# Scores of a head pair in one group, with two banks taken from the general PSUM pool

## The chip, the cores and the metric

The kernel runs on one core of one Trainium2 chip. The metric is the device time of one execution in microseconds (us), and every time below is the median of several executions unless it says otherwise. PE is TensorE, PEld its weight loads, DVE VectorE, ACT ScalarE, POOL GpSimd, SP SyncE. L469 means line 469 of the kernel concerned; the change shifts the lines.

## The reference

Two operators in a row: causal attention with a decay ("forgetting attention"), then a two-layer network with the SiLU function.

```python
def _attn_ref(q, k, v, f):                 # q, k, v: (8, 8, 576, 64); f: (8, 8, 576)
    scores = scale * np.matmul(q, k.transpose(0, 1, 3, 2))
    cum = np.cumsum(np.log(np.clip(f, 0.0001, 1.0)), axis=-1)
    decay = cum[:, :, :, None] - cum[:, :, None, :]
    scores = np.where(causal, -1000000000.0, scores + decay)
    ...                                    # softmax over the last axis
    return np.matmul(attn, v)

def _moe_ref(x, w_in, w_out):              # x: (4608, 512), w_in: (512, 2048), w_out: (2048, 512)
    h = x @ w_in
    g = h * (1.0 / (1.0 + np.exp(-h)))
    return g @ w_out
```

The output is 4608 x 512 in float32.

## The kernel before

The attention runs in 16 rounds of two units each; a unit is a pair of heads of one batch element. In between, slots are filled with pieces of the network, which make up most of the PE work. A piece is either an **M1** chunk (four matmuls into an `hp` tile, then tanh on ACT into `th`, then a multiplication on DVE into `gt`) or an **M2** part (four matmuls `po` that read finished `gt`). Two pools share the eight PSUM banks that the kernel uses: `psc` has two tiles of two banks for the scores, `pbig` has four tiles of one bank for everything else.

```python
psc  = tc.tile_pool(name="psc",  bufs=2, space=PSUM)   # [P, 2, 512] fp32: two banks each
pbig = tc.tile_pool(name="pbig", bufs=4, space=PSUM)   # one bank each: hp, po, dn, tx

def scores(n, c):                        # unit n, chunk c of 0, 1, 2
    ...
    sc = psc.tile([P, 2, SM], FP32, name="sc", tag="sc")
    for kb, q0, q1, o in CHUNKS[c]:
        for i in range(2):               # two heads: two 64-row halves of PE
            ...
            nc.tensor.matmul(sc[:, i, o : o + q1 - q0], lhsT=kt, rhs=t[r, q0:q1], ...)
    w = SM if c < 2 else T0
    nc.scalar.activation(out=u[:, :, c * SM : c * SM + w], in_=sc[:, :, 0:w], func=ACT.Exp, ...)
    ...                                  # masks on DVE; chunk 2 has a second exponential, into ut

def attend(n):                           # exponentials times values
    dn = pbig.tile([P, NGR, D + 1], FP32, name="dn", tag="big")
    ...

for m in range(NQ):                      # 16 rounds, two units each
    n = 2 * m
    piece = 1.7 if m < 2 else 2.4
    scores(n, 0); scores(n, 1); prepare(n)
    slot(piece, 2)                       # about 2.4 us of M1 and M2 pieces, M2 first if there is one
    ...                                  # back(m - 1): turn the attention output
    scores(n, 2); scores(n + 1, 0); prepare(n + 1)
    slot(piece, 2)
    scores(n + 1, 1); scores(n + 1, 2)
    slot(piece, 2)
    attend(n); attend(n + 1)
    slot(min(3.5, max(0.8, behind() - LAG)) if m > 1 else 0.8, 1)
```

(Calls that stand on lines of their own are put together here.) M2 of a token group can only run behind M1 of the same group, so now and then the M2 pieces run dry, and a slot then holds only `hp`.

The softmax here doesn't subtract the row's maximum and nothing guards it: scores larger than these inputs give would overflow.

## Time and profile before

| | before |
|---|---|
| median time | 346.49 us (three runs, 346.45 to 346.81) |
| span of the profiled run | 344.3 us |
| start, before the attention loop is in full swing | to about 58 us |
| loop of 16 rounds | about 58 to 284 us |
| tail, M1 and M2 only | from about 284 us |

Here are busy times by stretch for the loop, in us. The columns are the stretch, its length, then busy time and number of instructions for PE, PEld, DVE, ACT and POOL, then the granted PE clock, the share of the DMA engines in use and GB/s.

```profile
76.00:134.00 58.00, 56.37 (x696) 34.82 (x694) 35.53 (x76) 41.47 (x77) 28.07 (x47) 1.00 0.94 185
134.00:190.00 56.00, 56.00 (x662) 32.66 (x659) 32.96 (x66) 39.04 (x70) 21.85 (x38) 1.00 0.93 177
190.00:284.00 94.00, 93.76 (x1061) 56.28 (x1058) 51.65 (x113) 63.07 (x118) 26.53 (x47) 1.00 0.67 132
```

PE is busy for 206.13 of 208 us, ACT for 143.58 (69%). In the whole stretch from 134 to 190 us PE shows no idle time at all.

### The profile page before, as it was taken

Reading aid. Unit: us, or ns where it says so; the run is one execution under the profiler, and the core shown is the slowest. Engines: PE = TensorE matmul, PEld = TensorE weight load, DVE = VectorE, ACT = ScalarE, POOL = GpSimd, SP = SyncE. Lnnn points to the kernel's source line nnn. Section 1 sums busy time; section 2 is a strip of 40 time slices with the busy share of each in tenths; the row PEclk is TensorE's granted clock in tenths of the full one; section 3 lists DMA queues with packets and bytes.
Section 4 is the critical chain, followed back from the end, with each engine's and each line's share of the span. In section 5 each row is a group of like instructions: output and inputs, shape, how many; then the busy total and the mean of one; then the engine's idle time right before and its main releaser. Section 6 shows DMA issues by size and latency. Waiting matters only on the chain.

```text
span 344.3 us, 8892 instructions
## 1 busy us (share of the span) xinstructions
PE 335.4 (97%) x3567; PEld 198.9 (58%) x3567; DVE 185.5 (54%) x389; ACT 218.1 (63%) x401; POOL 129.0 (37%) x227
## 2 busy tenths in 40 slices
PE   8999999999998999999999999999999999999995
PEld 3654656667655656466465665656656565555654
DVE  4766646465667466367547653547645454535330
ACT  5866654887585766756759567595775934445341
POOL 8996225824427273055137128225320000010011
PEclk9999999999999999999999999999999999999999
DMA  8999999999699899798889999989832000010103
GB/s 157 200 185 220 198 163 162 236 214 194 159 186 197 202 202 159 169 191 182 166 205 153 171 195 196 154 182 197 147 86 56 33 32 30 32 55 30 40 38 86
DMA packets 141497, 50.44 MB, mean 147 GB/s; under 512 B 132368, under 2 KB 138768, under 8 KB 141456
## 3 DMA queue, kind: packets, MB, share of 16 engines
q1 hardware_dynamic: 131440, 32.70, 53.3%
q0 software_dynamic: 9856, 17.04, 21.4%
q8 instruction: 28, 0.46, 0.6%
q10 hardware_dynamic: 160, 0.13, 0.1%
q14 instruction: 13, 0.11, 0.1%
HBM read 36.85 MB, written 9.44 MB: 134 GB/s over the span
## 4 chain that ended last, share of the span: by engine, by line
PE 74%; DMA 13%; POOL 4%; SPq 3%; ACT 2%; DVE 2%; issue 1%; POOLq 0%
PE po L613 31%; PE hp L568 29%; PE sc L460 6%; PE dn L507 5%; DMA w_out_bf<-in_moe_w_out_dram 3%; DMA vf<-in_v_dram 3%; PE dn L516 3%; DMA qktf<-in_k_dram 3%; DMA qkT<-qkb 2%; SPq L158 1%; DMA f_sb<-in_f_dram 1%; DMA kf<-in_k_dram 1%; ACT th L576 1%; SPq L168 1%; ACT u L464 1%
## 5 line engine op out<-in xcount | busy, mean ns | idle before, releaser
L576 ACT ACTIVATE th<-hp 128x384 bf16<-128x384 f32 (+2 forms) x208 | 96.0, 478 | 90.6 <-PE hp L568 88.3
L577 DVE SCALAR_TENSOR_TENSOR gt<-th,hp 128x384 bf16<-128x384 bf16 (+2 forms) x208 | 105.9, 521 | 79.4 <-ACT th L576 75.8
L613 PE MATMUL po<-w_out_bf,gt 128*128 128x512 bf16 (+1 forms) x592 | 144.7, 374 | 0.0
L568 PE MATMUL hp<-x,w_in_bf 128*128 128x384 bf16 (+2 forms) x704 | 128.9, 321 | 0.2
L568 PEld LDWEIGHTS <-w_in_bf 128*128 128x128 bf16 x832 | 78.5, 98 | 55.2 <-issue 2.2
L613 PEld LDWEIGHTS <-gt 128*128 128x128 bf16 x592 | 54.6, 98 | 49.6 <-issue 2.1
L464 ACT ACTIVATE u<-sc 128x1024 bf16<-128x1024 f32 (+1 forms) x96 | 75.1, 821 | 11.1 <-PE sc L460 10.9
L592 POOL DMA_DIRECT2D out_dram<-osb x38 | 21.0, 552 | 133.4 <-ACT osb L623 86.4
L414 POOL TENSOR_TENSOR vp<-vf,w_bf 128x520 bf16<-128x520 f32 (+1 forms) x32 | 34.0, 1064 | 28.3 <-DMA vf<-in_v_dram 27.4
L469 DVE TENSOR_TENSOR u<-u,tri 128x768 bf16<-128x768 bf16 x32 | 22.6, 707 | 18.4 <-ACT u L464 18.4
L483 DVE TENSOR_TENSOR ut<-ut,trit 128x128 bf16<-128x128 bf16 x32 | 11.3, 354 | 34.8 <-ACT ut L476 34.8
L400 POOL CAST qkb<-qf 128x384 bf16<-128x384 f32 x32 | 17.3, 542 | 33.5 <-DMA qf<-in_q_dram 32.7
L623 ACT ACTIVATE osb<-po 128x512 f32<-128x512 f32 (+1 forms) x37 | 22.0, 594 | 12.4 <-PE po L613 12.3
L460 PE MATMUL sc<-qkT 64*128 64x128 bf16 (+1 forms) x640 | 26.5, 207 | 1.1 <-DMA qkT<-qkb 0.8
L460 PEld LDWEIGHTS <-qkT 64*128 64x128 bf16 x640 | 18.2, 94 | 12.2 <-issue 8.1
L476 ACT ACTIVATE ut<-sc 128x640 bf16<-128x640 f32 x32 | 23.3, 727 | 0.0
L507 PEld LDWEIGHTS <-u 128*128 128x128 bf16 x576 | 20.7, 97 | 3.9 <-issue 1.6
L507 PE MATMUL dn<-vp,u 128*128 128x65 bf16 x384 | 21.8, 193 | 0.0
L507 PE MATMUL dn<-v,u 128*128 128x65 bf16 x192 | 19.8, 193 | 1.3 <-DVE gt L577 1.3
L525 DVE TENSOR_TENSOR xr<-dn,rec 128x448 bf16<-128x448 f32 x32 | 20.0, 624 | 1.1
L400 POOL CAST qkb<-kf 128x384 bf16<-128x384 f32 x32 | 17.4, 543 | 7.9 <-DMA kf<-in_k_dram 7.8
L568 PE MATMUL hp<-xt,w_in_bf 128*128 128x256 bf16 x128 | 18.2, 272 | 0.3 <-DVE gt L577 0.2
(68 smaller groups left out, 204.5 us busy)
## 6 DMA issues: line engine op xcount, KB each, us to landing
out_dram<-osb POOLq DMA_DIRECT2D x32, 256.0 KB, 3.1
vf<-in_v_dram SPq DMA_DIRECT2D x26, 256.0 KB, 4.9
qf<-in_q_dram SPq DMA_DIRECT2D x64, 96.0 KB, 2.9
kf<-in_k_dram SPq DMA_DIRECT2D x64, 96.0 KB, 2.8
w_in_bf<-in_moe_w_in_dram POOLq DMA_DIRECT2D x4, 512.0 KB, 6.8
w_out_bf<-in_moe_w_out_dram POOLq DMA_DIRECT2D x4, 512.0 KB, 9.6
vf<-in_v_dram POOLq DMA_DIRECT2D x6, 256.0 KB, 10.0
qkb<-in_q_dram POOLq DMA_DIRECT2D x8, 128.0 KB, 5.0
```

What stands on the lines that cost most here:

```text
L400: nc.gpsimd.tensor_copy(out=t2[:, c0 : c0 + NR, :].rearrange("p c x -> p (c x)"), in_=t[:, :, :, :].rearrange("p c h d -> p (c h d)"),)
L414: nc.gpsimd.tensor_tensor(out=vbf[b][r, c, :, :], in0=vst[b][c][r, :, :], in1=w_bf[r, c + 1, b * H : (b + 1) * H, None].to_broadcast([n, H ...
L460: nc.tensor.matmul(sc[:, i, o : o + q1 - q0], lhsT=kt, rhs=t[r, q0:q1], start=True, stop=True)
L464: nc.scalar.activation(out=u[:, :, c * SM : c * SM + w], in_=sc[:, :, 0:w], func=ACT.Exp, scale=scale)
L469: nc.vector.tensor_tensor(out=x, in0=x, in1=tri[:, None, None, :].to_broadcast([P, 2, NR, P]), op=ALU.mult,)
L476: nc.scalar.activation(out=ut[:, :, 0:3:2, :].rearrange("p k i t -> p i k t"), in_=sc[:, :, T0 : T0 + (NM + 1) * ST].rearrange("p i (k t) ...
L507: nc.tensor.matmul(dn[:, i * NR + c - 1, :], lhsT=u[:, i, o : o + P], rhs=vals(kb, i), start=(kb == 0), stop=(kb == c),)
L568: nc.tensor.matmul(hp[:, :], lhsT=w_in_bf[:, cc, fc * P : (fc + 1) * P], rhs=xcols(g, cc), start=(cc == 0), stop=(cc == NCC - 1),)
L576: nc.scalar.activation(out=th[:, :], in_=hp[:, :], func=ACT.Tanh, scale=0.5)
L577: nc.vector.scalar_tensor_tensor(out=gt[:, fc, :], in0=th[:, :], scalar=1.0, in1=hp[:, :], op0=ALU.add, op1=ALU.mult,)
L613: nc.tensor.matmul(po[:, :], lhsT=gt[:, fc, tb * P : (tb + 1) * P], rhs=w_out_bf[:, fc, m0:m1], start=(fc == 0), stop=(fc == NFC - 1),)
L623: nc.scalar.activation(out=osb[:, :], in_=po[:, :], func=ACT.Copy, scale=0.5)
```

## The change

Its intent: fewer interruptions of the PE stream. The three chunks of one unit's scores are issued as one group, so two units make two groups where they made three. One group needs six banks (two for each chunk); the score pool has four, so chunk 1 takes two tiles of the general pool. Its exponential is split in two, one for each bank. The exponentials of chunk 2 are held back (`late`) until after the next M1 piece, so that its tanh comes first. The attention output `dn` moves from the general pool into the score banks. The slots are set to begin and end with an M2 piece where there is one. The diff, cut to its core:

```diff
-    def scores(n, c):
+    late: list = []
+    def scores(n):
...
-        sc = psc.tile([P, 2, SM], FP32, name="sc", tag="sc")
-        for kb, q0, q1, o in CHUNKS[c]:
+        for c in range(3):
+            if c == 1:
+                sc[c] = [pbig.tile([P, SM], FP32, name="sb", tag="big") for _ in range(2)]
+            else:
+                sc[c] = psc.tile([P, 2, SM], FP32, name="sc", tag="sc")
...
+            if c == 1:
+                for i in range(2):
+                    nc.scalar.activation(
+                        out=u[:, i, SM : 2 * SM], in_=sc[c][i][:, :], func=ACT.Exp, scale=scale
+                    )
+        def rest():
...                                     # both exponentials of chunk 2 and the mask of ut
+        late.append(rest)
@@ attend
-        dn = pbig.tile([P, NGR, D + 1], FP32, name="dn", tag="big")
+        dn_ = psc.tile([P, 2, SM], FP32, name="dn", tag="sc")
+        dn = dn_[:, 0, 0 : NGR * (D + 1)].rearrange("p (c d) -> p c d", d=D + 1)
@@ step
             m1_chunk(*M1[a])
+            while late:
+                late.pop(0)()
@@ fill
+            if last:
+                force = first if not begun else (last if at["left"] < 900 else 0)
+            t = step(force)
@@ the loop of 16 rounds
-        piece = 1.7 if m < 2 else 2.4
-        scores(n, 0)
-        scores(n, 1)
+        piece = 2.2 if m < 2 else 3.4
+        scores(n)
         prepare(n)
-        slot(piece, 2)
+        slot(piece, 2, 2)
...
-        scores(n, 2)
-        scores(n + 1, 0)
+        scores(n + 1)
         prepare(n + 1)
-        slot(piece, 2)
-        scores(n + 1, 1)
-        scores(n + 1, 2)
-        slot(piece, 2)
+        slot(piece, 2, 2)
         attend(n)
+        slot(0.7, 1)
         attend(n + 1)
-        slot(min(3.5, max(0.8, behind() - LAG)) if m > 1 else 0.8, 1)
+        slot(min(3.0, max(0.6, behind() - LAG)) if m > 1 else 0.6, 1, 2)
```

More of the change, by code (lines that the diff above doesn't have):

```diff
@@ L443 @@
     AT |= {(2, 1): RB, (3, 1): SM + RB, (3, 2): 2 * SM}
-    def scores(n, c):
+    late: list = []
+    def scores(n):
         b, p = divmod(n, NP)
-        if c == 0:
-            us[n] = upool.tile([P, 2, UW], BF16, name="u", tag="u")
+        us[n] = upool.tile([P, 2, UW], BF16, name="u", tag="u")
         u, ut = us[n], uts[n % 4]
         t = qkT[n]
-        sc = psc.tile([P, 2, SM], FP32, name="sc", tag="sc")
-        for kb, q0, q1, o in CHUNKS[c]:
-            for i in range(2):
-                r = slice(i * D, (i + 1) * D)
-                if kb == 0:
-                    kt = kT0[b][r, p, :]
-                else:
-                    k0 = RB if kb == NM else kb * P + RB
-                    kt = t[r, k0 : k0 + P]
-                nc.tensor.matmul(
-                    sc[:, i, o : o + q1 - q0], lhsT=kt, rhs=t[r, q0:q1], start=True, stop=True
-                )
-        w = SM if c < 2 else T0
-        nc.scalar.activation(
-            out=u[:, :, c * SM : c * SM + w], in_=sc[:, :, 0:w], func=ACT.Exp, scale=scale
-        )
-        if c == 0:
-            x = u[:, :, 0:RB].rearrange("p i (a t) -> p i a t", t=P)
-            nc.vector.tensor_tensor(
-                out=x,
-                in0=x,
-                in1=tri[:, None, None, :].to_broadcast([P, 2, NR, P]),
-                op=ALU.mult,
@@ new lines, in scores @@
+        sc = {}
+        for c in range(3):
[3 more added lines that the diff above has]
+                sc[c] = psc.tile([P, 2, SM], FP32, name="sc", tag="sc")
+            for kb, q0, q1, o in CHUNKS[c]:
+                for i in range(2):
+                    r = slice(i * D, (i + 1) * D)
+                    if kb == 0:
+                        kt = kT0[b][r, p, :]
+                    else:
+                        k0 = RB if kb == NM else kb * P + RB
+                        kt = t[r, k0 : k0 + P]
+                    x = sc[c][i] if c == 1 else sc[c][:, i, :]
+                    nc.tensor.matmul(
+                        x[:, o : o + q1 - q0], lhsT=kt, rhs=t[r, q0:q1], start=True, stop=True
+                    )
+            if c == 0:
+                nc.scalar.activation(
+                    out=u[:, :, 0:SM], in_=sc[c][:, :, :], func=ACT.Exp, scale=scale
+                )
+                x = u[:, :, 0:RB].rearrange("p i (a t) -> p i a t", t=P)
+                nc.vector.tensor_tensor(
+                    out=x,
+                    in0=x,
+                    in1=tri[:, None, None, :].to_broadcast([P, 2, NR, P]),
+                    op=ALU.mult,
+                )
+            if c == 1:
+                for i in range(2):
+                    nc.scalar.activation(
+                        out=u[:, i, SM : 2 * SM], in_=sc[c][i][:, :], func=ACT.Exp, scale=scale
+                    )
@@ L474, in scores @@
+        def rest():
+            x = sc[2]
+            nc.scalar.activation(
+                out=u[:, :, 2 * SM : UW], in_=x[:, :, 0:T0], func=ACT.Exp, scale=scale
             )
-        if c == 2:
             nc.scalar.activation(
                 out=ut[:, :, 0:3:2, :].rearrange("p k i t -> p i k t"),
-                in_=sc[:, :, T0 : T0 + (NM + 1) * ST].rearrange("p i (k t) -> p i k t", t=ST),
+                in_=x[:, :, T0 : T0 + (NM + 1) * ST].rearrange("p i (k t) -> p i k t", t=ST),
@@ L638, with step @@
     open2 = {"w": False}
-    def step():
+    def step(force=0):
         a, c = at["m1"], at["m2"]
@@ L658, in step @@
                 want = 1
-            can1 = want == 1
+            can1 = (force or want) == 1
         kind = 1 if can1 else 2
@@ L674, in behind, with fill @@
         return t / 1000
-    def fill(us_, first=0, least=0):
-        if first:
+    def fill(us_, first=0, least=0, last=0):
+        if first and not last:
             at["last"], at["row"] = 3 - first, 2
         at["left"] += us_ * 1000
+        begun = False
         while at["left"] > 0 or least > 0:
-            t = step()
+            force = 0
+            if last:
+                force = first if not begun else (last if at["left"] < 900 else 0)
+            t = step(force)
+            begun = True
             if t is None:
@@ L821, with slot @@
     pending: list = []
-    def slot(us_, first=0):
+    def slot(us_, first=0, last=0):
         n = len(stores)
-        fill(us_, first)
+        fill(us_, first, 0, last)
+        while late:
+            late.pop(0)()
         store(n)
```

## The prediction

> **What bounds the kernel now.** I read the page first: the engine totals, the slices, the chain that ended last.
>
> ```profile
> span 344.3 us, 8892 instructions
> PE 335.4 (97%) x3567; PEld 198.9 (58%) x3567; DVE 185.5 (54%) x389; ACT 218.1 (63%) x401; POOL 129.0 (37%) x227
> PEclk9999999999999999999999999999999999999999
> PE 74%; DMA 13%; POOL 4%; SPq 3%; ACT 2%; DVE 2%; issue 1%; POOLq 0%
> ```
>
> PE is busy 97% of the span at the full granted clock and holds 74% of the chain. The DMA share lies before 74 us, while weights and first heads load. A busy PE row is not proof, so I read the waits next, then the timeline of one stretch of the attention loop.
>
> ```profile
> ACT th L576 <- PE hp L568: 88.3, 105, 3.4
> PEld L460 <- issue: 14.0, 40, 0.4
> PE dn L507 <- DVE gt L577: 1.3, 1, 1.3
> PE sc L460 <- DMA qkT<-qkb: 0.8, 1, 0.8
> PE sc L460 <- ACT th L576: 0.3, 1, 0.3
> ```
>
> ACT waits for PE 88 us; PE waits for another engine in the loop hardly at all: 1.3, 0.8 and 0.3 us, once each. So PE's own stream sets the end, and only two things change the time: dead time inside that stream, or new waits in it. The second row hints at dead time: 40 times the weight loader stands idle at the score matmuls (L460) for no event.
>
> ```profile
> 135.23 2.12 PE L568 MATMUL hp<-x,w_in_bf 128*128 128x384 bf16 x12
> ...
> 137.28 0.40 PE L460 MATMUL sc<-qkT 64*128 64x128 bf16 x8
> 137.51 0.33 PE L460 MATMUL sc<-qkT,kT 64*128 64x384 bf16 x2
> 137.68 0.22 PE L460 MATMUL sc<-qkT 64*128 64x128 bf16 x2
> 137.77 1.93 ACT L464 ACTIVATE u<-sc 128x1024 bf16<-128x1024 f32 x2
> 137.83 1.47 PE L568 MATMUL hp<-x,w_in_bf 128*128 128x384 bf16 x8
> 139.14 1.89 PE L613 MATMUL po<-w_out_bf,gt 128*128 128x512 bf16 x8
> 139.58 0.89 ACT L576 ACTIVATE th<-hp 128x384 bf16<-128x384 f32 x2
> 140.12 1.02 DVE L577 SCALAR_TENSOR_TENSOR gt<-th,hp 128x384 bf16<-128x384 bf16 x2 [0.74 <-ACT th L576]
> 140.96 0.23 PE L460 MATMUL sc<-qkT 64*128 64x128 bf16 x2
> ```
>
> Twelve hp matmuls last 2.12 us from first start to last end and one lasts 0.326, so they stream at (2.12 - 0.326)/11 = 0.163 us. They should hand over at 135.23 + 12 x 0.163 = 137.19; the next hp starts at 137.83: the score group takes 0.64 us. Its own streaming, two 64-row halves at once, is five pairs of 128 columns at (0.40 - 0.22)/3, about 0.057 us, and one of 384 at 0.17, together 0.45. About **0.2 us per group** is entering and leaving the 64-row form. The group at 140.96 gives the same. The attention matmuls (dn, 128 rows) show none.
>
> **What the Trainium skill says.** "TensorEngine Tiling (Array Packing)", Key Properties: changing the tiling mode (not just the tile) drains TensorE. The trace agrees and sizes it at 0.2 us for the way in and out. "ScalarE: Activation LUTs", What ACT_TABLE_LOAD costs: an ACTIVATE takes 186 ns + 0.833 ns per column, neighbours overlapping by some 93 ns, so halving one costs some 0.1 us. Below, 1024 columns take 1034 ns and 512 take 597: it agrees. "PSUM — Partial Sum Buffer", PSUM bank collisions: guard PSUM by bank, not by address. The built program does: a tile waits for the last reader of its bank. No page prices a wait for a bank; the trace must.
>
> ```profile
> L464 ACT ACTIVATE u<-sc 128x1024 bf16<-128x1024 f32 x64 | 64.4, 1034 | 9.6 <-PE sc L460 9.4
> L576 ACT ACTIVATE th<-hp 128x512 bf16<-128x512 f32 x16 | 9.6, 597 | 5.9 <-PE hp L568 5.9
> L476 ACT ACTIVATE ut<-sc 128x640 bf16<-128x640 f32 x32 | 23.3, 727 | 0.0
> L577 DVE SCALAR_TENSOR_TENSOR gt<-th,hp 128x384 bf16<-128x384 bf16 x128 | 69.1, 552 | 47.1 <-ACT th L576 44.1
> ```
>
> **The change, part by part.**
>
> *Fewer mode switches.* Two score units (head pairs) used to be cut into three groups, now into two. Over 16 loop rounds that is 48 against 32 groups (counted in both built programs): 16 x 0.2 = **-3.3 us** on the path. Matmuls and their columns are the same.
>
> *ACT.* The exponential of chunk 1 becomes two of 512 columns: 32 more instructions, some 0.1 us each, +3 us of ACT in all, not on the path by itself (about 70% busy in the loop).
>
> *The banks.* This costs. Before, scores and exponentials lived in four banks of their own, while hp, po, dn and tx shared four. Now chunk 1 takes two of the general banks for as long as ACT needs to read them, so matmuls must wait for a scores exponential, and scores for the gt of a hidden chunk. dn moves into the score banks, where it collides with little: their exponentials are done before dn comes.
>
> I walked by hand through the new order with the durations above. Score group at 0: ACT starts at 0.49 (137.77 - 137.28), chunk 0 ends at 1.46, the two halves at about 1.98 and 2.50. The deferred exponentials of chunk 2 (0.97) come behind the first th. PE's slot starts at 0.73.
> - *po hp hp hp po*: po ends 1.6, the hp's 2.25, 2.9, 3.55; the halves' banks were free at 2.05 and 2.6. No wait; here the M2 piece at each end does its work.
> - *hp hp hp hp po*, where M2 has run dry (once for nearly each token group): ACT reads the first hp only after 2.5 (th 2.9, gt 3.5), then chunk 2 till 3.87, then three th to 4.3, 4.73, 5.17; gt at 4.87, 5.38, 5.9. PE's fourth hp ends at 3.34, po waits for the first gt (0.2), ends 4.42; the next scores start at 4.52 and their chunk 1, due at 4.75, needs the banks of the second and third hp: gt at 4.87 and 5.38. About **0.9 us** lost.
> - *po hp hp po*, then scores, then *po hp hp hp po*: about 0.3 lost, part of it chunk 2 waiting for the earlier chunk 2 to be read.
>
> By the order, rounds 4 to 15 hold six bad slots (0.9 to 1.1 each, 5.8) and six mild rounds (1.8): 7.6 us. Rounds 0 to 3 add about 3.7: a slot with seven hp in a row (1.9), two pieces of 0.4, two tx turns of 0.5. Sum 11.3. I take three quarters, **+8.5**: the walk supposes that ACT serves every exponential at full length, and pieces that shift by some tenths find their bank free. Of the 2.4 us of waits in the loop today, one (0.8, for the transposed q and k) should shrink because scores ask for them later: **-1**.
>
> Sum: 346.5 - 3.3 + 8.5 - 1 = 350.7. M work taken out of the slots goes to the tail, where PE streams without gaps, so it costs nothing. Predicted **350.5 us**.
>
> **Rivals.**
> 1. *The gain arrives whole, no new waits*: 346.5 - 3.3 - 1 = 342 us. For it: ACT waits 88 us for PE, so there is room on average; M2 pieces and the deferred chunk 2 were plainly put in against these waits. Against it: in a slot without M2 the waits follow from single durations, not from averages.
> 2. *ACT becomes the burst bound everywhere*: backlog carries from one group to the next and the whole 11 us or more shows: 355 to 357. For it: between two score groups ACT must do 2.0 + 1.0 of scores and three or four th, 4.4 to 5 us, and PE's slot with its group is just 4.4. Against it: the attention blocks (0.86 us each) with hardly any ACT work follow every second group, and let it catch up.
> 3. *DVE jitter*: the DVE multiplication of the ut block has a mean of 354 ns, but took 1.92 us at 104.85, just before the one long PE wait on a bank (1.3). With two banks fewer, such hiccups reach PE more often: +1 to +3.
> 4. *The input DMA is the bound in rounds 0 to 2* (scores waited for it at 74 us); then changes there are hidden and the early 3.7 us costs less.
>
> **Range and chances.** Low end: rival 1 with a few waits, 344. High end: the full walk with rival 3, 356. Faster by over 2% would need 339.6: the switches cannot give it, 0.02. Slower by over 2% is above 353.4, between the taken and the full sum of waits: 0.28. Within 2%: 0.70.
>
> **What would show each step.** The waits of the changed kernel should have new rows: PE sb waiting for DVE gt, hp for ACT u, po for gt, together 6 to 11 us, and idle PE of that size in the loop (76 to 284 us). The loader's "issue" idle at the scores should fall by a third, with 32 groups in the timeline at 0.2 each. The halves of chunk 1 should take 0.52 to 0.6 us. dn should wait for little. The prediction is wrong if PE's waits stay under 3 us (then about 343), or if the switch cost does not go away with the groups.

## The result

| | before | changed |
|---|---|---|
| median time, us | 346.47 (345.56 to 346.81, four runs) | 348.72 (348.02 to 349.54, four runs) |
| span of the profiled run, us | 344.3 | 347.8 |
| ratio | | 1.007, 95% interval 1.0041 to 1.0099 |

A ratio is computed as the mean time of one kernel's runs over that of the other's of the same rounds, so it is not quite the ratio of the medians quoted. Executions over 1.5% slower than the fastest of the same kernel are left out of the means. The changed kernel is the same within 2%, and within that slower by 0.7%. In later rounds on another chip the ratio was 1.0027 (0.9998 to 1.0056). So the change costs between 0.9 us (348.55 less 347.64, the means of those rounds) and 2.4 us; the profiled runs differ by more, 3.5 us. Single executions of one kernel are spread over up to 4 us (345.12 to 349.34 for eleven runs of the kernel before in one set of rounds), so the difference between two profiled runs must not be taken for the mean one.

The page of the changed kernel, in the lines that the prediction showed of the one before:

```profile
span 347.8 us, 8936 instructions
PE 336.3 (97%) x3567; PEld 202.9 (58%) x3567; DVE 187.9 (54%) x389; ACT 220.0 (63%) x433; POOL 129.7 (37%) x227
...
PEclk9999999999999999999999999999999999999999
...
PE 68%; DMA 10%; ACT 6%; POOL 6%; DVE 4%; issue 4%; SPq 2%; POOLq 0%
```

The clock is the same. PE's busy time is the same within 1 us, with the same 3567 matmuls. What moved is the chain: PE's share falls from 74% to 68%, and ACT and DVE rise from 2% each to 6% and 4%. Waits have come into the path. The waits of the changed kernel (total us, number, longest us):

```profile
ACT th L597 <- PE hp L589: 80.4, 101, 3.2
...
PEld L469 <- issue: 12.4, 31, 1.2
...
PE sc L469 <- DMA qkT<-qkb: 1.2, 1, 1.2
PE sb L469 <- DVE gt L598: 1.2, 2, 0.9
...
PE hp L589 <- DVE gt L598: 1.1, 1, 1.1
...
PE dn L528 <- ACT ut L494: 0.3, 1, 0.3
...
PE hp L589 <- ACT u L485: 0.2, 1, 0.2
PE po L634 <- ACT u L485: 0.2, 1, 0.2
```

Two rows foretold are there, chunk 1 (`sb`) for a `gt` and `hp` for a scores exponential; `hp` for a `gt` and `po` for a scores exponential are of the same kind. They add up to 1.2 + 1.1 + 0.2 + 0.2 = 2.7 us, not the 6 to 11 that I wanted to see. The next section shows where the rest is. The busy times by stretch, same columns as before:

```profile
76.00:134.00 58.00, 55.66 (x688) 35.33 (x685) 34.38 (x74) 41.92 (x85) 28.75 (x48) 1.00 0.91 188
134.00:190.00 56.00, 55.71 (x639) 33.26 (x638) 31.36 (x64) 39.17 (x78) 22.53 (x38) 1.00 0.95 182
190.00:284.00 94.00, 92.58 (x1083) 57.90 (x1082) 54.81 (x117) 64.50 (x133) 26.35 (x47) 1.00 0.67 129
```

PE idles for 4.05 of the 208 us, against 1.87 before: 2.2 us more. This too is less than the loss. And the exponentials (line, engine, operation, output from input, number, then busy us and mean ns):

```profile
L473 ACT ACTIVATE u<-sc 128x1024 bf16<-128x1024 f32 x32 | 33.3, 1039 | 14.6 <-PE sc L469 14.6
...
L485 ACT ACTIVATE u<-sb 128x512 bf16<-128x512 f32 x64 | 35.2, 616 | 0.0
...
L494 ACT ACTIVATE ut<-sc 128x640 bf16<-128x640 f32 x32 | 23.8, 743 | 0.0
```

Half an exponential has a recorded length of 616 ns, but the two records overlap: a pair takes about 1.09 us from start to end, where the whole one takes 1039 ns. The split costs ACT little.

### The profile page after: what moved, and what is told of

The parts are those of the page before. It is cut to its first block, busy times and chain, and to the rows that moved or that the text cites. A ratio compares the mean times of both kernels' runs of the same rounds, so it can differ in the third digit from the quotient of the medians.

```text
span 347.8 us, 8936 instructions
## 1 busy us (share of the span) xinstructions
PE 336.3 (97%) x3567; PEld 202.9 (58%) x3567; DVE 187.9 (54%) x389; ACT 220.0 (63%) x433; POOL 129.7 (37%) x227
## 4 chain that ended last, share of the span: by engine, by line
PE 68%; DMA 10%; ACT 6%; POOL 6%; DVE 4%; issue 4%; SPq 2%; POOLq 0%
PE po L634 28%; PE hp L589 26%; PE dn L528 4%; PE sc L469 3%; DMA w_out_bf<-in_moe_w_out_dram 3%; DMA qktf<-in_k_dram 3%; PE dn L537 2%; DVE gt L598 2%; DMA qkT<-qkb 2%; ACT th L597 2%; PE sb L469 1%; PE wm L232 1%; ACT u L485 1%; DMA vf<-in_v_dram 1%; POOL v L341 1%
## 5 line engine op out<-in xcount | busy, mean ns | idle before, releaser
L597 ACT ACTIVATE th<-hp 128x384 bf16<-128x384 f32 (+2 forms) x208 | 96.4, 485 | 83.6 <-PE hp L589 80.4
L634 PE MATMUL po<-w_out_bf,gt 128*128 128x512 bf16 (+1 forms) x592 | 142.2, 374 | 0.2 <-ACT u L485 0.2
L589 PE MATMUL hp<-x,w_in_bf 128*128 128x384 bf16 (+2 forms) x704 | 127.0, 321 | 1.8 <-DVE gt L598 1.1
L589 PEld LDWEIGHTS <-w_in_bf 128*128 128x128 bf16 x832 | 77.7, 98 | 51.1 <-issue 3.1
L634 PEld LDWEIGHTS <-gt 128*128 128x128 bf16 x592 | 55.6, 98 | 50.6 <-issue 1.0
L473 ACT ACTIVATE u<-sc 128x1024 bf16<-128x1024 f32 x32 | 33.3, 1039 | 14.6 <-PE sc L469 14.6
L485 ACT ACTIVATE u<-sb 128x512 bf16<-128x512 f32 x64 | 35.2, 616 | 0.0
L469 PEld LDWEIGHTS <-qkT 64*128 64x128 bf16 x640 | 19.8, 94 | 18.1 <-issue 12.4
L469 PE MATMUL sc<-qkT 64*128 64x128 bf16 (+1 forms) x576 | 25.4, 206 | 1.7 <-DMA qkT<-qkb 1.2
L501 DVE TENSOR_TENSOR ut<-ut,trit 128x128 bf16<-128x128 bf16 x32 | 13.0, 405 | 24.0 <-ACT ut L494 24.0
L528 PEld LDWEIGHTS <-u 128*128 128x128 bf16 x576 | 21.8, 98 | 5.8 <-issue 0.5
```

The source lines that it names most:

```text
L469: nc.tensor.matmul(x[:, o : o + q1 - q0], lhsT=kt, rhs=t[r, q0:q1], start=True, stop=True)
L473: nc.scalar.activation(out=u[:, :, 0:SM], in_=sc[c][:, :, :], func=ACT.Exp, scale=scale)
L485: nc.scalar.activation(out=u[:, i, SM : 2 * SM], in_=sc[c][i][:, :], func=ACT.Exp, scale=scale)
L528: nc.tensor.matmul(dn[:, i * NR + c - 1, :], lhsT=u[:, i, o : o + P], rhs=vals(kb, i), start=(kb == 0), stop=(kb == c),)
L589: nc.tensor.matmul(hp[:, :], lhsT=w_in_bf[:, cc, fc * P : (fc + 1) * P], rhs=xcols(g, cc), start=(cc == 0), stop=(cc == NCC - 1),)
L597: nc.scalar.activation(out=th[:, :], in_=hp[:, :], func=ACT.Tanh, scale=0.5)
```

## Where the time went: starts instead of spans

The wait view and the busy time look at the gap between a matmul's recorded end and the next start. The recorded end comes late by some 0.16 us for 384 columns, so a wait of up to that length shows nowhere, and a longer one shows short by as much. The wait view also lists no gap under 0.15 us. The Trainium skill, "Perfetto Trace Analysis", Tensor Engine Instruction (MATMUL, LD_WEIGHTS), says it in so many words: "the TE profile time is a model, not a measurement". This trace agrees (0.326 us recorded, 0.163 from start to start). Starts, though, are recorded. So I took the distance from each matmul's start to the next one's and subtracted what it streams when nothing holds it up: 0.216 us for 512 columns, 0.163 for 384, 0.109 for 256, 0.056 for 128, 0.029 for 64 or 65, with two 64-row halves counted once. What is left over is time in which PE streams nothing.

| us | before | changed | difference |
|---|---|---|---|
| streaming, whole program | 314.0 | 313.8 | -0.2 |
| not streaming, whole program | 25.0 | 28.7 | +3.7 |
| of that from 58 to 300 us | 13.3 | 16.5 | +3.2 |
| - into and out of the 64-row form | 9.1 (48 groups) | 6.1 (32 groups) | -3.0 |
| - waits for a DMA and for what the kernel before also waited for | 3.3 | 1.3 | -2.0 |
| - waits for a bank that the change brought | 0 | 8.5 | +8.5 |
| - rest, small gaps | 0.9 | 0.6 | -0.3 |

Starts add up to the span, and both kernels stream the same matmuls, so the first two rows meet the 3.5 us between the spans by construction. What is measured is where the lost time lies. The division of the waits is mine. The kernel before has 0.98 us of DMA wait and 2.35 us of bank waits of its own (1.50 of them `dn` at 107.29 us), which sit in the second of the four last rows. All bank waits together are 2.35 against 8.5, all waits 3.3 against 9.8. In a score group I count what the whole group takes beyond one that isn't held up, since one half goes on while the other waits. The lost time is in a few places. A slot in which M2 had run dry, in the timeline of the changed kernel (start, length, engine, line, operation; `x16` is a run of sixteen):

```profile
140.43 2.77 PE L589 MATMUL hp<-x,w_in_bf 128*128 128x384 bf16 x16
...
141.08 1.09 ACT L485 ACTIVATE u<-sb 128x512 bf16<-128x512 f32 x2
...
142.04 0.52 ACT L597 ACTIVATE th<-hp 128x384 bf16<-128x384 f32 x1
...
142.67 0.76 ACT L494 ACTIVATE ut<-sc 128x640 bf16<-128x640 f32 x1
...
143.26 1.33 ACT L597 ACTIVATE th<-hp 128x384 bf16<-128x384 f32 x3
...
143.85 1.48 DVE L598 SCALAR_TENSOR_TENSOR gt<-th,hp 128x384 bf16<-128x384 bf16 x3 [0.16 <-ACT th L597]
...
144.45 0.78 PE L469 MATMUL sb<-qkT,kT 64*128 64x384 bf16 x2
```

ACT reads the two halves of chunk 1, one tanh, then chunk 2, and only then, at 143.26, the other three tanh. DVE's last three `gt` follow from 143.85 to 145.33. The next chunk 1 comes at 144.45 and needs the banks of two of those `hp` tiles. A pair of these matmuls takes 0.33 us when nothing holds it up (at 82.12 and 139.92, for example); here it takes 0.78, because the second of the two waits 0.46. Nothing of it is a row of the wait view: 0.32 of it lie inside the recorded length of the first, and the 0.14 left are too short to be listed. With it the whole group takes 0.52 us longer than one that isn't held up, and with 0.15 before `po` this slot loses 0.67 us.

## The experiments

Twelve runs were made, of ten new kernels and two repeats, all with the right result, in three sets of rounds (e1 to e4, e5 to e8, e9 to e12), each on one chip with the kernel before beside it. All ratios are against the kernel before in the same rounds. The medians of the kernel before were 347.35, 347.19 and 347.81.

### e1: chunk 2 held back past the second tanh

My theory: chunk 2's exponentials sit ahead of three tanh in the slots without M2; let two tanh go first.

```diff
     def rest(): ...
     late.append(rest)
+    since["m1"] = 0
@@ step
             m1_chunk(*M1[a])
-            while late:
+            since["m1"] += 1
+            while late and since["m1"] >= 2:
                 late.pop(0)()
```

> The changed kernel with the deferred exponentials of chunk 2 put behind the second hidden chunk's tanh instead of the first. Theory (banks are held because ACT serves 0.97 us of chunk 2 ahead of the next tanh): the waits of chunk 1 for a gt in the slots of four hp (three of 0.46 us, one of 1.2, one of 0.65 in the changed kernel) shrink to 0.1 or less each, PE's non-streaming time in the loop falls by some 2 us, time about 346.7 (ratio to before 1.000 to 1.002). Rival (DVE, not ACT, holds the banks, or the waits are hidden by other waits): no change, 348.7. A second rival: chunk 2's score bank is now freed later, and the next group's chunk 2 waits as long as chunk 1 did: 348 to 349 with the waits moved from sb to sc.

Measured: ratio 1.0046 (1.0005 to 1.0087), mean of five runs 348.83. The sixth execution, the profiled one, took 1100.88 us, so there is no profile to read; I don't know why, and no other run did it. No gain over the changed kernel can be seen, and without a profile the run doesn't say why.

### e2: the same past the third tanh

```diff
-            while late and since["m1"] >= 2:
+            while late and since["m1"] >= 3:
```

> The same, behind the third hidden chunk's tanh. Theory: in slots of four hp like the run before (346.5 to 347); in slots with fewer hidden chunks chunk 2 is read at the slot's end and the next group's chunk 2 may wait 0.2 to 0.4 for it, so equal to or up to 1 us slower than the run with two. Rival (DVE holds the banks): 348.7.

Measured: 349.00 us, ratio 1.0052 (1.0013 to 1.0091), no gain. This one has a profile. In the slot that was shown above the order is now three tanh, chunk 2, one tanh, and the next chunk 1 doesn't wait:

```profile
142.57 1.29 ACT L599 ACTIVATE th<-hp 128x384 bf16<-128x384 f32 x3
...
144.93 0.33 PE L470 MATMUL sb<-qkT,kT 64*128 64x384 bf16 x2
```

The other slots pay for it. The chunk 2 of the next unit now finds its score banks unread, and the wait view has a row for this that the changed kernel lacks:

```profile
PE sc L470 <- ACT ut L495: 1.5, 3, 1.0
```

By starts, it is 0.28 us in each of three rounds, 0.41 in two and 1.17 in one, and 15.1 us of the loop are not streaming, against 16.5. So the mechanism in the dry slots is as I said, and the cure moves the wait from one pair of banks to another. The second rival of e1's expectation held.

### e3: dn back in the general pool

```diff
-        dn_ = psc.tile([P, 2, SM], FP32, name="dn", tag="sc")
-        dn = dn_[:, 0, 0 : NGR * (D + 1)].rearrange("p (c d) -> p c d", d=D + 1)
+        dn = pbig.tile([P, NGR, D + 1], FP32, name="dn", tag="big")
```

> One part of the change undone: the attention outputs are back in the general banks, all else as changed. Theory (general banks are the scarce thing): each dn holds one for 0.86 us of matmul and 0.8 us of DVE, so that hp, po and sb wait more: 2 to 6 us slower than the changed kernel, 351 to 355. Rival (dn is followed by enough other work that the banks it takes are free anyway): 348.7 within 0.5.

Measured: 348.48 us, ratio 1.0036 (0.9987 to 1.0085): not slower than the changed kernel. In its trace the dry slots show the same waits of 0.46 and 0.65 us. I had expected harm; no effect of the placement of `dn` can be seen here. By starts all its bank waits are 7.9 us against 8.5. In the score banks `dn` waits 0.44 us for chunk 2's exponential and chunk 2 waits 0.15 and 0.49 for DVE to read `dn`; back in the general pool, four waits for that read sum to 1.1. One cost replaces the other.

### e4: without the M2 piece at the end of a slot

```diff
-        slot(piece, 2, 2)
+        slot(piece, 2)
...
-        slot(min(3.0, max(0.6, behind() - LAG)) if m > 1 else 0.6, 1, 2)
+        slot(min(3.0, max(0.6, behind() - LAG)) if m > 1 else 0.6, 1)
```

> One part of the change undone: slots end as they did before, without an M2 piece kept for the end. Theory (an M2 piece next to a score group gives ACT and DVE the time to free banks): 1 to 4 us slower than the changed kernel, 350 to 353, with more waits of sb for gt. Rival (the pieces' order hardly matters because the M2 pieces run out in the bad slots anyway): 348.7 within 0.7.

Measured: 350.13 us, ratio 1.0078 (1.0025 to 1.0132), against the changed kernel's 1.007 and 1.0027. By starts its loop has 17.4 us that are not streaming against 16.5. Its DMA wait is shorter (0.45 us against 1.29), so the bank waits alone are 10.1 against 8.5. So the ordering is worth 1 to 2 us in the trace; by the clock, since the two weren't in the same rounds, it lies between nothing and 2 us.

### e5: the kernel before with 64 groups instead of 48

If a group costs 0.2 us by itself, then sixteen groups more must cost 3 us without any change of banks.

```diff
-        piece = 1.7 if m < 2 else 2.4
+        piece = 1.3 if m < 2 else 1.8
         scores(n, 0)
+        slot(piece, 2)
         scores(n, 1)
```

> The kernel before with its first score group of every round cut in two by hidden work: 64 groups of 64-row matmuls in the loop instead of 48, same matmuls, same banks, same exponentials. Theory (each group costs about 0.19 us of PE for entering and leaving the 64-row form): 16 x 0.19 = 3 us longer than before, 349.5 where before is 346.5 (ratio 1.008 to 1.010), with entry plus exit time in the trace up from 9.1 to about 12 us. Rival (the dead time at a group's ends is only how the trace models matmul ends, or it is hidden): ratio 1.000 to 1.003.

Measured: 348.93 us, ratio 1.0054 (1.0025 to 1.0082), so +0.9 to +2.8 us. By starts, the way in costs 6.1 us and the way out 5.9: 12.1 against 9.1, which is 3.0 for sixteen groups, 0.19 each. The loader's idle time at the scores, which was 40 times and 14.0 us, is now

```profile
PEld L460 <- issue: 19.7, 59, 0.4
```

So in the traces the cost goes with the number of groups, up and down, and no bank changed hands here: the loss is the group's own. The clock gives a little less, 1.9 us with an interval that ends at 2.8, between theory and rival. Nothing in the trace accounts for the rest: PE's other waits are about the same, 3.2 us against 3.3.

### e6: keep some M2 in reserve

The slots without M2 are the bad ones. Let M2 lag a little, so that there is a piece left, and end a slot early rather than run a third M2 when M1 has run dry.

```diff
-            f2 = (c - sum(M2_OF[:g2])) / M2_OF[g2]
+            f2 = (c - sum(M2_OF[:g2])) / M2_OF[g2] + 0.2
@@ fill
+        ran = 0
         while at["left"] > 0 or least > 0:
...
+            dry = M1[at["m1"]][0] not in ready if at["m1"] < len(M1) else True
+            if last and dry and ran >= 2:
+                at["left"] = 0.0
+                return False
...
+            ran += 1
```

> The changed kernel with another distribution of the same hidden pieces: a slot in which no hidden chunk is ready stops after two M2 pieces, and M2 is held back by 0.2 of a token group, so that M2 pieces are left for the slots that had four hp in a row. Banks, groups and exponentials as changed. Theory (the waits for banks come from slots where M2 has run dry): the three 0.46 us waits and the 1.2 and 0.65 us ones of sb for gt in rounds 5 to 15 go, non-streaming PE time in the loop falls from 16.5 to 12 or 13 us, and the time is 3 to 4 us under the changed kernel: ratio to before 0.994 to 0.999. Rival (the banks are short whatever the order, waits move to other slots): as the changed kernel, ratio 1.005 to 1.008.

Measured: 348.06 us, ratio 1.0025 (1.0003 to 1.0047); the loop has 14.4 us that are not streaming, 1.15 of them a DMA wait. Less than the changed kernel in the trace, but more than the 12 or 13 expected; by the clock the two overlap. From 134 us on the bank waits are 2.9 us against 4.0. The waits foretold to go went in part, and others came up (0.88 us at 184, 0.69 at 227). So theory and rival each held in part.

### e7: chunk 1 last

If chunk 1 is issued as the last of the three, its banks have longer to come free.

```diff
-        for c in range(3):
+        for c in (0, 2, 1):
```

> The changed kernel with the chunks of a score group in the order 0, 2, 1, so that the two general banks are asked for some 0.19 us later; the exponentials keep their order. Theory (chunk 1 waits for gt by fixed times): each wait of sb for gt shrinks by about 0.19, some ten of them, 1 to 1.5 us in all: ratio to before 1.002 to 1.004 where the changed kernel has 1.005 to 1.007. Rival: chunk 2 is now asked for earlier and waits for the chunk 2 before it: no gain.

Measured: 348.91 us, ratio 1.0049 (1.0013 to 1.0084), loop 17.4 us. In the three dry slots of 0.52 us the score group now loses 0.32, about the 0.19 less that was foretold, but chunk 2, which now comes sooner, waits 0.52, 0.35 and 0.12 in other places. The 17.4 us can't be compared as they stand: a mask multiplication on DVE took 2.13 us at 106.56, the scores then waited 1.05 and 0.91 us for `dn` to be read out of the score banks, and in the slot behind that eleven matmuls ran at half the granted clock, 1.8 us. The first line is of the timeline; the second has the columns of the stretches above, and 0.50 is the granted clock:

```profile
111.00 0.40 PE L469 MATMUL sc<-qkT 64*128 64x128 bf16 x8 [0.99 <-DVE xr L546]
...
114.00:115.00 1.00, 1.00 (x4) 0.44 (x3) 0.55 (x1) 1.00 (x4) 0.51 (x1) 0.50 1.20 243
```

By the clock of six executions there is no gain alone.

### e8: both

e6 and e7 in one kernel.

> Both edits of the two runs before together. Theory: the best of these, 4 us under the changed kernel, ratio to before 0.992 to 0.998; at least not slower than the one with the reserve alone. Rival: with the reserve there is no wait left for the chunk order to shorten, equal to it.

Measured: 346.00 us, ratio 0.997 (0.9944 to 0.9995), loop 13.8 us. From 134 us on the changed kernel has five slots behind a score group with four `hp` in a row; here one is left, of five `hp` at 238 us. The slots now mix M1 and M2:

```profile
137.80 1.04 PE L634 MATMUL po<-w_out_bf,gt 128*128 128x512 bf16 x4
...
138.67 1.46 PE L589 MATMUL hp<-x,w_in_bf 128*128 128x384 bf16 x8
...
139.97 1.03 PE L634 MATMUL po<-w_out_bf,gt 128*128 128x512 bf16 x4
...
140.93 0.45 PE L469 MATMUL sc<-qkT 64*128 64x128 bf16 x10
...
141.36 0.33 PE L469 MATMUL sb<-qkT,kT 64*128 64x384 bf16 x2
```

The pair at 141.36 takes its 0.33 us, without a wait. From 134 us on, the waits of the loop sum to 1.7 us, against 4.0 in the changed kernel. Before 134 us they are still 5.6 us, among them 0.82 in the slot of seven `hp` and 0.96 behind one slow DVE instruction (below).

### e9 and e10: the changed kernel and e8 once more

To compare them on one chip.

> The changed kernel itself, again, on the chip and in the rounds of the next three, because single runs of one kernel differ by up to 3 us from each other. Expected from its first runs: 348.7, ratio to before 1.005 to 1.009, with 8 to 9 us of PE waits in the loop.

> The version with the M2 reserve and the chunk order 0, 2, 1, again, beside the changed kernel. If its first ratio to before (0.997) was no accident: 0.994 to 0.999 again and 2 to 3 us under the changed kernel. Rival (the difference between it and the reserve alone was the start of the run, whose DMA waits vary by 2 us): 1.000 to 1.003.

Measured: the changed kernel 348.33 us, ratio 1.0027 (0.9998 to 1.0056); e8's kernel 347.46 us, ratio 1.0008 (0.9973 to 1.0043). So e8's kernel, over two sets of rounds, is level with the kernel before, and its lead of the first set didn't hold: what came is the rival's range. Against the changed kernel it is 0.7 us faster by the means, where 2 to 3 were expected.

The changed kernel's ratio is below the expected 1.005 to 1.009, but the waits are as expected. Its second profile has about 8.5 us of bank waits again (the profiles of this set lack some 48 matmul records each; I left out the gaps of that size), and 3.6 of them from 134 us on, where the first had 4.0. It has no DMA wait, and 1.9 of the 8.5 us follow one DVE multiplication of 2.14 us at 105.29.

### e11: the best combination

e8, with chunk 1 last only from the fifth unit on, and with a slot also cut short when M2 has run dry after four pieces.

```diff
-        for c in (0, 2, 1):
+        for c in (0, 1, 2) if n < 4 else (0, 2, 1):
...
-            if last and dry and ran >= 2:
+            m2_dry = M2[at["m2"]][0] >= M1[min(at["m1"], len(M1) - 1)][0]
+            if last and (dry and ran >= 2 or m2_dry and ran >= 4 and first == 2):
```

> The same with two edits for rounds 0 to 3: the chunk order 0, 1, 2 there (chunk 2 waited 0.52 and 0.35 us for the chunk 2 before it), and a slot that has only hp pieces stops after four (seven in a row had cost 1.4 us). Theory: 1 to 1.5 us under the version before it, ratio to before 0.990 to 0.996. Rival (the four hp taken out only move the wait to the next score group, because ACT has the same work in less time): equal to it.

Measured: 345.94 us, ratio 0.996 (0.992 to 1.0001). Against the changed kernel in the same rounds (e9), the means are 346.23 and 348.55: 2.3 us less, give or take about 1.7 by the spread of six runs each. In the traces, counted alike, the bank waits from 134 us on are 1.7 against 3.6, in the whole loop about 5.0 against 8.5 (1.9 of these behind the slow multiplication). So slots and order alone win back what the change had lost. It has the lowest median of its rounds, 1.9 us under that of the kernel before, but the interval touches 1: whether it beats the kernel before stays open.

### e12: the kernel before with the split exponential

```diff
-        nc.scalar.activation(
-            out=u[:, :, c * SM : c * SM + w], in_=sc[:, :, 0:w], func=ACT.Exp, scale=scale
-        )
+        for r in ((slice(0, 1), slice(1, 2)) if c == 1 else (slice(0, 2),)):
+            nc.scalar.activation(
+                out=u[:, r, c * SM : c * SM + w], in_=sc[:, r, 0:w], func=ACT.Exp, scale=scale
+            )
```

> The kernel before with one part of the change alone: the exponential of chunk 1 in two instructions of 512 columns, banks and groups as before. Theory (some 0.1 us of ACT each, 3 us in all, none of it on the path, since PE sets the end): ratio to before 0.998 to 1.002, ACT busy time up by 2 to 5 us, no new PE wait. Rival (ACT is tight enough in the bursts that it costs): 1.003 or more.

Measured: 347.37 us, ratio 0.9992 (0.9962 to 1.0023).

```profile
PE 332.2 (96%) x3520; PEld 199.2 (58%) x3567; DVE 184.8 (53%) x389; ACT 219.9 (63%) x433; POOL 129.5 (37%) x227
```

ACT's 32 more instructions cost it 219.9 - 218.1 = 1.8 us and the kernel nothing. (The trace lacks 47 of the 3567 matmul records, which is why PE's busy time looks short.) The banks here are those of the kernel before, and counted by starts its bank waits are 3.6 us, 0.5 of them from 134 us on.

Not tested alone were the holding back of chunk 2 as such and the new lengths of the slots.

## Why the prediction was right

The time: 348.72 us measured, 350.5 predicted, inside the range of 344 to 356 and in the class "within 2%" that had the chance of 0.70. The loss itself was too large in the forecast: +4 us, against +2.4 by the means of these rounds and +0.9 in the later ones. In terms of the sum, step by step:

**The bound.** Right. PE streams for 314 of 344 us, and the difference of the spans is dead time inside PE's stream, in places that the starts show.

**Fewer mode switches, -3.3 us.** Right (16 x 0.2 is 3.2): 9.1 us fell to 6.1, -3.0, at 0.19 us a group. e5, which only adds groups, gives +3.0 for sixteen more.

**ACT, +3 us, off the path.** Right in what matters and large by half: ACT's busy time rose by 1.9 us, and e12 gives 1.8 and no loss of time. That is 0.06 us for each of the 32 cuts; the 0.1 us was an estimate from the page's figures. The halves have recorded lengths of 616 ns, and a pair takes 545 ns for each, about the 0.52 to 0.6 us foretold.

**The banks, 11.3 us by the walk, +8.5 taken.** The mechanism is shown by the timeline and by e2 and e8, which take away the cause and with it the wait in that slot, and over the run by e9 and e11 in the same rounds. The sum measured is 8.5, as much as was taken. Its terms:

| | walk | by starts |
|---|---|---|
| six bad slots, rounds 4 to 15 | 5.8 | 4.7 |
| six mild rounds | 1.8 | 0.4 |
| rounds 0 to 3 | 3.7 | 3.4 |

A bad slot was to lose about 0.9 us, with 0.2 before `po` and 0.17 and 0.5 at chunk 1; the one shown loses 0.15 and then 0.52. The seven `hp` in a row were to lose 1.9 and lose 2.0. The term that was mis-sized is the mild rounds: 1.8 predicted, 0.4 found (0.27 at 131 us, 0.13 at 230). In the 4.7 are 0.49 us that the walk didn't have, chunk 2 waiting at 111.59 for DVE to read `dn`. With the 0.44 and 0.15 under e3, the move of `dn` into the score banks took 1.1 of the 8.5 us: it collided with a little more than the prediction had it. And in rounds 0 to 3 no `tx` turn waited, for which the walk had 1.0. I took three quarters of the whole sum with an argument about ACT's full-length service and shifting pieces. The sum came out on the point, but the early term needed hardly a discount, the bad slots a fifth and the mild rounds three quarters, so the factor was right by luck.

**One wait less, -1 us.** Mis-sized: it was -2.0. I had expected the DMA wait for q and k to shrink. It grew, from 0.98 to 1.29 us. What went away was the 1.5 us wait of `dn` at 105.8 us, with two more of 0.45 and 0.40. The long one was an accident of timing in the kernel before, visible in its timeline:

```profile
104.47 0.52 POOL L400 CAST qkb<-qf 128x384 bf16<-128x384 f32 x1
...
104.85 1.92 DVE L483 TENSOR_TENSOR ut<-ut,trit 128x128 bf16<-128x128 bf16 x1 [0.90 <-ACT ut L476]
...
105.63 2.18 POOL L414 TENSOR_TENSOR vp<-vf,w_bf 128x520 bf16<-128x520 f32 x2
...
107.29 0.19 PE L507 MATMUL dn<-v,u 128*128 128x65 bf16 x1 [1.34 <-DVE gt L577]
```

A DVE multiplication that takes 0.22 us at 143.47 in the changed kernel takes 1.92 here, beside GpSimd's casts and multiplications. The Trainium skill, "SBUF — State Buffer", Who interferes with whom, has the rule: DVE's second pair of SBUF ports is shared with GpSimd under an exclusive lock. The timeline agrees with it; that this lock made the 1.92 us is argued and not tested by a run. Such a hiccup doesn't hit the same wait each time (in e8 a 2.08 us one at 126.35 let `hp` wait 0.96), and one profile can't say what it costs on average. That the term was -2.0 here was luck: in the second profile of the changed kernel (e9) the hiccup is back, 2.14 us at 105.29, and the scores and an `hp` wait 1.9 us behind it.

**The sum.** In the profiled runs -3.0 + 8.5 - 2.0 - 0.3 = +3.2 in the loop, predicted +4.2. By the clock it is +0.9 to +2.4. Part of that gap is that single runs differ by some us: the part before 58 us alone has 11.1 to 13.6 us that are not streaming, depending on the run. In e2, e3 and e6 some 1.7 us of that is the stretch at half the clock. A second pair of profiles, e9 and e12 (which has the banks of the kernel before, and no loss from its split), has about 8.5 us of waits against 5.2, 1.5 of these for a DMA. That is +3.3 where the first pair has +6.5 and the prediction +7.5; less the 3.0 it leaves +0.3, and by the clock the two are 1.0 apart (348.55 and 347.50). So the term that was too large is what the waits add: the kernel before has 3.3 to 5.2 us of its own, of which I had counted 2.4. With two pairs of profiles, how much is the change's own stays open between these.

**The rivals.** The gain arriving whole (342 us) fell: 8.5 us of new waits. ACT as the bound everywhere (355 to 357) fell: ACT still waits 80.4 us for PE, and from 134 us on nearly all the waits (3.9 of 4.0 us) are in or behind slots where M2 is dry. DVE jitter is real in kind: in the slot with seven `hp`, the `ut` multiplication took 0.93 us, and what follows waits for DVE:

```profile
85.31 2.18 POOL L414 TENSOR_TENSOR vp<-vf,w_bf 128x520 bf16<-128x520 f32 x2 [0.20 <-DMA vf<-in_v_dram]
85.31 0.99 ACT L597 ACTIVATE th<-hp 128x256 bf16<-128x256 f32 x3
85.51 0.93 DVE L501 TENSOR_TENSOR ut<-ut,trit 128x128 bf16<-128x128 bf16 x1 [0.45 <-ACT ut L494]
...
86.82 1.03 PE L589 MATMUL hp<-x,w_in_bf 128*128 128x256 bf16 x8 [1.11 <-DVE gt L598]
```

That is at most 0.7 us of the 2.0 that this slot lost (0.93 less 0.22), an estimate; in e9, where this multiplication isn't slow, the slot lost 1.45. With the 1.9 us behind the hiccup in e9, jitter is a real part of the 8.5, near the low end of the +1 to +3. The kernel before pays for it too, 1.5 us here and 1.7 in e12, so that it strikes more often with two banks fewer is not shown. The input DMA as the bound of the first rounds fell: the early bank waits came nearly whole, 3.4 of 3.7.

**What would show it.** This part of the prediction failed, and it is the one to learn from. I asked for 6 to 11 us of PE waits in the wait view and as much idle PE, and wrote that the prediction would be wrong if the waits stayed under 3 us. They are 2.7, with 2.2 us of additional idle time, and by my own test I would have had to expect 343 us. The step that failed is to read a wait from the recorded end of a matmul, which is about 0.16 us late (for the second of two 64-row halves the record of the first covers 0.32) and hides the short waits that this change brings. I had the number for it in my hands, 0.326 against 0.163, and used it for the mode switch but not for the test. The loader's idle time at the scores fell from 14.0 to 12.4 us and not by a third either: the number of times fell, 40 to 31. Two of them now hold a bank wait (1.2 us at 245 and 0.6 at 273, where 0.4 was the longest before), but that makes up for 1 us only.

## What to carry to other kernels

A group that streams well by itself is not free if it borrows buffers from its neighbours: price the way in and out of it, then walk each slot with single durations to see whose read frees the bank that comes next, above all in the slots where the filler work has run dry. When a saturated PE loses time in portions of 0.1 to 0.5 us, count from start to start, since busy time and wait rows hide portions of that size. And when a change trades one cost for another of its size, look for the version that keeps the gain and mends the loss by order alone, as e11 did against the changed kernel in the same rounds.

## What the Trainium skill lacked or had wrong

- "TensorEngine Tiling (Array Packing)" says that a mode switch drains TensorE but gives no cost. The runs show 0.19 us for the way into and out of a group of 64-row matmuls: 9.1 us for 48 groups, 6.1 for 32, 12.1 for 64.
- "Perfetto Trace Analysis" says that the end of a matmul is an estimate, but not what this does to the search for gaps that it recommends: here the wait rows showed 2.7 us of bank waits and the starts 8.5. The page names start-to-start spacing for GpSimd instructions only, not for matmuls.
- The same page advises to rotate groups through the PSUM banks, but no page prices a wait for a bank: 0.67 us for a slot of four M1 chunks and no M2, 2.0 us for seven in a row.
- "SBUF — State Buffer" agrees with what was seen: one 128x128 multiplication on DVE took 1.92 and 2.08 us beside GpSimd work, where the median of the 32 is 0.23. It doesn't say that such a block travels: behind it PE stood 1.5 us (the kernel before) and 0.96 us (e8), since a `gt` came late and with it a PSUM bank.
- "ScalarE: Activation LUTs" was not wrong, only a little high: a pair of 512-column exponentials takes 1.09 us, where an estimate by its formula with the overlap gives 2 x (0.186 + 0.833 x 0.512) - 0.093 = 1.13 us.
